# Mixture of experts on one core: the row gathers move from beside the first products to behind the output steps

## The chip, the cores and the metric

The kernel runs on one core of a Trainium2 chip. The metric is the device time of one execution in microseconds (us). Its engines are TensorE (PE in the profile; PEld are its weight loads), VectorE (DVE), ScalarE (ACT), GpSimd (POOL) and SyncE (SP). SP issues the plain DMAs, POOL the indirect ones, which gather or scatter rows by a list of indices.

## The reference, cut to what matters

Three layers follow each other: a linear attention, a dense two-layer network, and a mixture of 8 experts of which each of 2304 tokens takes two. The change lies in the last one.

```python
N, D, E, F = (2304, 512, 8, 1024)
noisy_logits = x @ w_gate + np.log1p(np.exp(x @ w_noise)) * noise
top2 = ...            # the two largest of the 8, and their softmax weights top2_w
out = np.zeros((N, D))
for e in range(E):
    for k in range(2):
        mask = top2[:, k] == e
        h = np.maximum(x[mask] @ w1[e], 0.0)
        out[mask] += top2_w[mask, k, None] * (h @ w2[e])
```

## The kernel before

The attention and the dense layer run first, in groups of 512 tokens. Their result, the token rows x, is written to a DRAM buffer `x2d`. While they run, the router of each group writes every token's number and weight into the list of its expert (36 small indirect DMAs, line 799, each followed by a memset named spacer). An expert's list has a capacity of CAP = 640 tokens, five blocks of 128.

The expert stage then works through the experts in order, lines 1095 to 1124. All products are float32 made of three float32r matmuls (`mm3`, lines 170 to 175): high x high, high x low, low x high. For expert e there are two phases.

- *First products* (`h2_step`, lines 888 to 904): for each of eight f, 128 hidden units by 640 tokens, as two parts of 384 and 256 columns with 12 matmuls each. They go to one of two PSUM buffers (`py`, tag Y). ACT writes the high part of the activated product to `hTh` (line 902), DVE the low part to `hTl` (line 903). PE's product f+2 needs the buffer of product f, so it waits for both.
- *Output steps* (`y2_step`, lines 908 to 927): for each block j of 128 tokens, 24 matmuls of 512 columns into one of two PSUM accumulators (`pa`, tag A). ACT scales them by the token's weight into a tile `y2s` (line 916), and POOL adds that tile to the output rows with an indirect DMA (line 917) and then writes the spacer (line 919).

Rows come in by `gather` (line 862). For experts 2 to 7 a block of 128 tokens takes four indirect DMAs on POOL (line 866), each of 128 rows of 512 bytes, into a tile of the pool `gp`, which has six buffers. `gtrans` (line 875) transposes a block on DVE and splits it into high and low (ACT line 885, DVE line 161). The transposition of expert e+1's block j stands ahead of expert e's output step j (line 1118), so the rows of expert e+1 are used in the output phase of expert e.

The program's order is written out by hand (`manual_schedule`), and each engine runs its own instructions in that order. At the top of expert e's turn stand the 20 gathers of expert e+1 (lines 1097 to 1099) and the loads of w1 for expert e+1 (SP, line 818); then the eight first products, with the split of w2 behind every second one; then the loads of w2 for expert e+1 (SP, line 822); then the five output steps. On POOL this gives, for each expert, 20 gathers in one run and then five pairs of scatter and spacer, each pair waiting for its output step. A scatter of expert e also waits for the adds of expert e-1 to land (lines 924 to 926).

Of the kernel before, what the change touches and what calls it, by code (L numbers as in the profile page):

```python
# [38 lines left out]
def attn_moe_moe2_kernel(  # L39
# [19 lines left out]
    E, _, F2 = w1.shape  # L59
# [10 lines left out]
    NB = CAP // P  # L70
# [80 lines left out]
    def GG(shape, dt, name):  # L151
        return gp.tile(shape, dt, tag="G", name=name)

    def TT(shape, dt, name):
        return tp.tile(shape, dt, tag="T", name=name)
# [14 lines left out]
    def mm3(out_ap, stat, mov, ssl, msl, start, stop):  # L170
        sh, sl = stat
        mh, ml = mov
        nc.tensor.matmul(out_ap, sh[ssl], mh[msl], start=start, stop=False)  # L173
        nc.tensor.matmul(out_ap, sh[ssl], ml[msl], start=False, stop=False)  # L174
        nc.tensor.matmul(out_ap, sl[ssl], mh[msl], start=False, stop=stop)  # L175
# [640 lines left out]
    def load_w1(e, i):  # L816
        raw1[e, i] = (HH if e == 0 else SS)([P, F2], F32, f"w1_{e}_{i}")
        nc.sync.dma_start(out=raw1[e, i], in_=quads(w1[e], i) if e >= NE else w1[e, i * P:(i + 1) * P, :])

    def load_w2(e, i):  # L820
        raw2[e, i] = SS([P, 2, DM], F32, f"w2_{e}_{i}")
        nc.sync.dma_start(out=raw2[e, i], in_=w2[e, 2 * i * P:2 * (i + 1) * P, :].rearrange("(a p) c -> p a c", p=P))

    def split_w1(e, i):
        s1[e, i] = split(W, raw1[e, i], [P, F2], f"s1_{e}_{i}")

    def split_w2(e, i):
        s2[e, i] = split(W, raw2[e, i], [P, 2, DM], f"s2_{e}_{i}", nc.gpsimd if e == 0 and i < 2 else None)
# [33 lines left out]
    def gather(e, j):  # L862
        if e >= NE:
            t = GG([P, NQ, P], F32, f"xg{e}_{j}")
            for g in range(NQ):
                nc.gpsimd.indirect_dma_start(out=t[:, g, :], out_offset=None, in_=x2d.rearrange("n (i c) -> (n i) c", c=P),  # L866
                                             in_offset=bass.IndirectOffsetOnAxis(ap=lq[:, e - NE, j, g:g + 1], axis=0))
        else:
            t = (HH if e == 0 and j < EB else GG)([P, DM], F32, f"xg{e}_{j}")
            rows = P + (groups[-1][0] if j < EB else NT)  # L870
            nc.gpsimd.indirect_dma_start(out=t, out_offset=None, in_=x2d[0:rows, :],
                                         in_offset=bass.IndirectOffsetOnAxis(ap=lst[:, e, j, 2:3], axis=0))
        xg[e, j] = t

    def gtrans(e, j):
        if j == 0:
            xgT[e] = (XX([P, NPR, CAP], F32R, f"xgh{e}"), XX([P, NPR, CAP], F32R, f"xgl{e}"))
        if e >= NE:
            t = quarters_transposed(xg[e, j], f"xgt{e}_{j}")
        else:  # L880
            t = MM([P, NPR, P], f"xgp{e}_{j}")
            for c in range(NPR):
                nc.tensor.transpose(t[:, c, :], xg[e, j][:, c * P:(c + 1) * P], ident)
        hi, lo = (u[:, :, j * P:(j + 1) * P] for u in xgT[e])
        nc.scalar.copy(hi, t)
        split_lo(lo, t, hi)

    def h2_step(e, f, parts=HALVES):
        if len(parts) == 2:
            ps = py.tile([P, 2, DM], F32, tag="Y", name=f"h2_{e}_{f}")  # L890
            banks = [ps[:, i, :] for i in range(2)]
        else:
            banks = [pa.tile([P, DM], F32, tag="A", name=f"h2_{e}_{f}_{parts[0][0]}")]
        for (a, n), bk in zip(parts, banks):
            for c in range(NPR):
                mm3(bk[:, :n], s1[e, c], xgT[e], (slice(None), slice(f * P, (f + 1) * P)),
                    (slice(None), c, slice(a, a + n)), c == 0, c == NPR - 1)
        if (e, f // 2) not in hT:
            hT[e, f // 2] = (HH([P, 2, CAP], F32R, f"hTh{e}_{f}"), HH([P, 2, CAP], F32R, f"hTl{e}_{f}"))
        for (a, n), bk in zip(parts, banks):  # L900
            hi, lo = (t[:, f % 2, a:a + n] for t in hT[e, f // 2])
            nc.scalar.activation(hi, bk[:, :n], AF.Relu)  # L902
            nc.vector.scalar_tensor_tensor(out=lo, in0=bk[:, :n], scalar=0.0, in1=hi.bitcast(F32),  # L903
                                           op0=ALU.max, op1=ALU.subtract)
# [3 lines left out]
    def y2_step(e, j, between={}):  # L908
        ps = pa.tile([P, DM], F32, tag="A", name=f"y2_{e}_{j}")
        for f in range(NF2):  # L910
            mm3(ps, tuple(t[:, f % 2] for t in hT[e, f // 2]), s2[e, f // 2], (slice(None), slice(j * P, (j + 1) * P)), (slice(None), f % 2),
                f == 0, f == NF2 - 1)
            if f in between:
                between[f]()
        t = TT([P, DM], F32, f"y2s{e}_{j}")
        nc.scalar.activation(t, ps, AF.Copy, scale=lst[:, e, j, 1:2].bitcast(F32))  # L916
        i = nc.gpsimd.indirect_dma_start(out=out, out_offset=bass.IndirectOffsetOnAxis(ap=lst[:, e, j, 0:1], axis=0),  # L917
                                         in_=t, in_offset=None, compute_op=ALU.add)
        nc.gpsimd.memset(spacer, 0)


        for o in adds.get(e, []):
            tc.declare_no_dep(i.ins, o.ins, reason="a token has one slot of an expert")
        for o in adds.get(e - 1, []):
            tc.add_manual_dep(i.ins, o.ins.name, mybir.DependencyInfo(mybir.DependencyClass.Sync, mybir.DependencyReason.DATA),
                              reason="adds to the same rows")
        adds.setdefault(e, []).append(i)


    with tc.manual_schedule():  # L930
# [164 lines left out]
        for e in range(E):  # L1095
            nx = e + 1 < E
            if nx and e:
                for j in range(NB):
                    gather(e + 1, j)
                for i in range(NPR):  # L1100
                    load_w1(e + 1, i)
            for f in range(NF2):
                h2_step(e, f, HALVES if e else PARTS[1:])
                if e and f % 2 == 0:
                    split_w2(e, f // 2)
                if e == 0 and f % 2:
                    gtrans(1, f // 2)
            if nx:
                for i in range(NF2 // 2):
                    load_w2(e + 1, i)  # L1110
            for j in range(NB):
                if e == 0 and j < EB - 1:
                    continue
                if nx:
                    if e:
                        if j < NPR:
                            split_w1(e + 1, j)
                        gtrans(e + 1, j)
                    elif j == EB - 1:
                        for i in range(NPR):  # L1120
                            split_w1(1, i)
                    else:
                        gtrans(1, j)
                y2_step(e, j)
    work.close()


# [69 lines left out]
```

## Time and profile before

| what | us |
|---|---|
| median of 3 runs | 1051.83 |
| lowest and highest of them | 1051.07, 1052.28 |
| the profiled execution's own time | 1058.36 |
| its span, first to last instruction | 1056.7 |
| mean granted TensorE clock in it | 0.952 of full speed |

| engine | busy us | share | instructions |
|---|---|---|---|
| PE | 968.6 | 92% | 4897 |
| DVE | 553.7 | 52% | 978 |
| ACT | 427.1 | 40% | 688 |
| POOL | 293.9 | 28% | 342 |

How to read it: a row of a timeline gives an instruction's start, its duration, the engine, the line of the kernel, the operation, what it writes and reads, and in square brackets the idle time of the engine ahead of it with what ended that idle time. "issue" there means that the profile shows nothing that the engine waited for, "remote" that an unknown one released it. The ends of matmuls are modelled. A row of the table of stretches gives, for each engine, its busy time in the stretch and the number of its instructions, then the granted clock (1.00 is 2.4 GHz), the busy share of the DMA engines and the GB/s that they moved.

### The profile page before, as it was taken

The page shows a single profiled execution, that of the slowest core. Times are in us where ns is not written, and L with a number is a line of the kernel's source. Part 1 is how long each engine was busy: PE and PEld are TensorE (multiplying, and loading weights), DVE is VectorE, ACT ScalarE, POOL GpSimd, SP SyncE. Part 2 cuts the span into 40 slices and gives each one's busy share as a digit, 9 for nine tenths or more (in the row PEclk, how much of TensorE's full clock was granted, in tenths as well). Part 3 has the DMA queues.
Part 4 walks back from the last instruction along what each step waited for, and adds up shares of the span by engine and source line. Part 5 has one row for each costly group of instructions (what it writes and reads, how often), then busy time and mean ns, then how long its engine had stood idle before and what let it go on. Part 6 is the DMA issues. An engine that isn't in the chain of part 4 may idle for free.

```text
span 1056.7 us, 12905 instructions
## 1 busy us (share of the span) xinstructions
PE 968.6 (92%) x4897; PEld 818.0 (77%) x4897; DVE 553.7 (52%) x978; ACT 427.1 (40%) x688; POOL 293.9 (28%) x342
## 2 busy tenths in 40 slices
PE   7989799999999999999999599697996997969994
PEld 7457578888888888898789499686886886868993
DVE  7899947964795567568434143242432523325320
ACT  3756544634463445467424132232331422314320
POOL 4002100150024003106342515427145162361111
PEclk8999899999999999999999799899898998989998
DMA  7688508600800120030652335244252442522203
GB/s 208 199 234 210 68 1 190 209 2 18 177 17 1 46 55 1 1 120 22 239 137 70 120 85 125 70 117 113 71 120 80 113 127 62 126 92 61 31 11 41
DMA packets 107282, 100.08 MB, mean 95 GB/s; under 512 B 58320, under 2 KB 82896, under 8 KB 107216
## 3 DMA queue, kind: packets, MB, share of 16 engines
q1 hardware_dynamic: 95664, 78.17, 26.2%
q0 software_dynamic: 11552, 21.04, 10.6%
q8 instruction: 40, 0.66, 0.3%
q14 instruction: 26, 0.21, 0.1%
HBM read 78.46 MB, written 20.72 MB: 94 GB/s over the span
## 4 chain that ended last, share of the span: by engine, by line
PE 74%; DVE 9%; issue 6%; another core or an unknown queue 5%; ACT 4%; DMA 1%; POOL 0%; DVEq 0%; POOLq 0%; SPq 0%; ACTq 0%
PE y L174 12%; PE y L173 12%; PE y L175 12%; PE h L175 11%; PE h L173 11%; PE h L174 10%; PE xp L495 2%; DVE stage L566 2%; ACT hTh L902 1%; PE kvp L381 1%; DVE hTl L903 1%; DVE stage L565 1%; PE qTp L482 1%; DVE hs L613 1%
## 5 line engine op out<-in xcount | busy, mean ns | idle before, releaser
L903 DVE SCALAR_TENSOR_TENSOR hTl<-h,hTh 128x384 fp32r<-128x384 f32 (+3 forms) x128 | 62.8, 491 | 233.7 <-ACT hTh L902 168.3
L902 ACT ACTIVATE hTh<-h 128x384 fp32r<-128x384 f32 (+3 forms) x128 | 56.0, 438 | 228.4 <-PE h L175 83.2
L917 POOL DMA_INDIRECT out_dram<-y2s,lst x40 | 63.3, 1581 | 282.9 <-ACT y2s L916 282.6
L866 POOL DMA_INDIRECT xg<-x2d,lq x120 | 118.9, 991 | 35.9 <-issue 33.1
L613 DVE SCALAR_TENSOR_TENSOR hs<-hs 128x512 f32<-128x512 f32 (+1 forms) x80 | 55.2, 690 | 54.5 <-ACT hs L612 52.7
L173 PE MATMUL h<-xgh,s_0h 128*128 128x384 f32 (+3 forms) x128 | 43.9, 343 | 43.1 <-DVE hTl L903 25.0
L438 POOL TENSOR_TENSOR q<-q,qm 128x1024 f32<-128x1024 f32 (+1 forms) x10 | 18.2, 1818 | 209.3 <-DVE qm L437 132.0
L612 ACT COPY hs<-h 128x512 f32<-128x512 f32 (+1 forms) x80 | 43.3, 541 | 76.7 <-PE h L175 73.1
L916 ACT ACTIVATE y2s<-y,lst 128x512 f32<-128x512 f32 x40 | 27.6, 689 | 91.3 <-PE y L175 76.4
L799 POOL DMA_INDIRECT lstd<-rrow,rsi x36 | 43.3, 1201 | 67.5 <-DVE rsi L796 61.6
L173 PEld LDWEIGHTS h<-xgh,s_0h 128*128 128x128 f32 x128 | 25.7, 201 | 46.9 <-DVE hTl L903 27.8
L624 ACT CAST g<-hs 128x512 fp32r<-128x512 f32 (+1 forms) x72 | 41.3, 573 | 37.8 <-DVE hs L613 37.7
L161 DVE TENSOR_TENSOR g<-hs,g 128x512 fp32r<-128x512 f32 (+1 forms) x72 | 44.9, 624 | 0.5 <-ACT g L624 0.5
L175 PE MATMUL h<-xgh,s_3l 128*128 128x384 f32 (+3 forms) x128 | 41.2, 322 | 2.9 <-issue 2.6
L175 PE MATMUL h<-xgh,s_0l 128*128 128x384 f32 (+3 forms) x128 | 41.9, 327 | 1.9 <-issue 1.9
L173 PE MATMUL h<-xgh,s_1h 128*128 128x384 f32 (+3 forms) x128 | 41.8, 327 | 1.7 <-issue 1.5
L174 PE MATMUL h<-xgl,s_0h 128*128 128x384 f32 (+3 forms) x128 | 42.1, 329 | 1.3 <-issue 1.3
L174 PE MATMUL h<-xgl,s_2h 128*128 128x384 f32 (+3 forms) x128 | 41.6, 325 | 1.1 <-issue 1.1
L173 PE MATMUL h<-xgh,s_2h 128*128 128x384 f32 (+3 forms) x128 | 41.4, 323 | 1.3 <-issue 1.3
L175 PE MATMUL h<-xgh,s_1l 128*128 128x384 f32 (+3 forms) x128 | 41.3, 323 | 1.3 <-issue 1.3
L174 PE MATMUL h<-xgl,s_1h 128*128 128x384 f32 (+3 forms) x128 | 41.5, 324 | 0.9 <-issue 0.8
L175 PE MATMUL h<-xgh,s_2l 128*128 128x384 f32 (+3 forms) x128 | 41.5, 324 | 0.6 <-issue 0.6
(341 smaller groups left out, 2914.4 us busy)
## 6 DMA issues: line engine op xcount, KB each, us to landing
w<-in_moe_w_dram SPq DMA_DIRECT2D x64, 512.0 KB
stage<-in_moe_w_in_dram SPq DMA_DIRECT2D x16, 512.0 KB
stage<-in_moe_w_out_dram SPq DMA_DIRECT2D x16, 512.0 KB
out_dram<-zero SPq DMA_DIRECT2D x1, 4864.0 KB
x2d<-x2s SPq DMA_DIRECT2D x9, 512.0 KB
k<-in_k_dram SPq DMA_DIRECT2D x12, 256.0 KB
v<-in_v_dram SPq DMA_DIRECT2D x12, 256.0 KB
x2q<-x2d SPq DMA_DIRECT2D x24, 128.0 KB
```

What stands on the lines that cost most here:

```text
L161: (eng or nc.vector).tensor_tensor(out=lo, in0=src, in1=hi.bitcast(F32), op=ALU.subtract)
L173: nc.tensor.matmul(out_ap, sh[ssl], mh[msl], start=start, stop=False)
L174: nc.tensor.matmul(out_ap, sh[ssl], ml[msl], start=False, stop=False)
L175: nc.tensor.matmul(out_ap, sl[ssl], mh[msl], start=False, stop=stop)
L612: nc.scalar.copy(hs, ps)
L613: nc.vector.scalar_tensor_tensor(out=hs, in0=hs, scalar=0.01, in1=hs, op0=ALU.mult, op1=ALU.max)
L624: nc.scalar.copy(parts[0], hs)
L799: i = nc.gpsimd.indirect_dma_start(out=lstd, out_offset=bass.IndirectOffsetOnAxis(ap=si[:, kk, r:r + 1], axis=0), in_=row[:, kk, r, :], in ...
L866: nc.gpsimd.indirect_dma_start(out=t[:, g, :], out_offset=None, in_=x2d.rearrange("n (i c) -> (n i) c", c=P), in_offset=bass.IndirectOffse ...
L902: nc.scalar.activation(hi, bk[:, :n], AF.Relu)
L903: nc.vector.scalar_tensor_tensor(out=lo, in0=bk[:, :n], scalar=0.0, in1=hi.bitcast(F32), op0=ALU.max, op1=ALU.subtract)
L917: i = nc.gpsimd.indirect_dma_start(out=out, out_offset=bass.IndirectOffsetOnAxis(ap=lst[:, e, j, 0:1], axis=0), in_=t, in_offset=None, com ...
```

## The change

The gathers of expert 2 stay where they were, at the top of expert 1's turn. Those of expert e+2, for e from 1 to 5, are issued in expert e's output phase instead of at the top of the turn of expert e+1: the four gathers of block j stand behind output step j of expert e, that is behind its scatter and spacer on POOL. Nothing else moves.

```diff
         for e in range(E):
             nx = e + 1 < E
             if nx and e:
-                for j in range(NB):
-                    gather(e + 1, j)
+                if e == 1:
+                    for j in range(NB):
+                        gather(2, j)
                 for i in range(NPR):
                     load_w1(e + 1, i)
             for f in range(NF2):
...
                     else:
                         gtrans(1, j)
                 y2_step(e, j)
+                if e and e + 2 < E:
+                    gather(e + 2, j)
     work.close()
```

## Rows read from the trace of the kernel before

**Rows 1.** The page: span, busy time by engine, and the evacuation of an output step.
```profile
span 1056.7 us, 12905 instructions
PE 968.6 (92%) x4897; PEld 818.0 (77%) x4897; DVE 553.7 (52%) x978; ACT 427.1 (40%) x688; POOL 293.9 (28%) x342
...
L916 ACT ACTIVATE y2s<-y,lst 128x512 f32<-128x512 f32 x40 | 27.6, 689 | 91.3 <-PE y L175 76.4
```

**Rows 2.** Table of stretches, each from one expert's first output scatter to the next's.
```profile
625.28:693.50 68.22, 59.01 (x314) 53.25 (x313) 24.15 (x34) 20.83 (x35) 28.54 (x30) 0.92 0.39 100
...
899.03:967.29 68.26, 58.91 (x314) 52.80 (x313) 24.14 (x34) 20.84 (x35) 28.41 (x30) 0.92 0.38 99
967.29:1022.65 55.36, 55.36 (x314) 50.66 (x313) 21.69 (x31) 19.11 (x32) 8.51 (x11) 1.00 0.18 25
sum 397.37, PE 351.73 PEld 317.07 DVE 142.41 ACT 123.40 POOL 150.72; mean PE 58.62 PEld 52.85 DVE 23.74 ACT 20.57 POOL 25.12
```

**Rows 3.** Timeline of ACT: three first products of expert 3, high part.
```profile
726.00 0.49 ACT L902 ACTIVATE hTh<-h 128x384 fp32r<-128x384 f32 x1 [3.22 <-PE h L175]
...
738.17 0.49 ACT L902 ACTIVATE hTh<-h 128x384 fp32r<-128x384 f32 x1 [9.73 <-issue]
...
746.03 0.49 ACT L902 ACTIVATE hTh<-h 128x384 fp32r<-128x384 f32 x1 [6.36 <-remote]
```

**Rows 4.** Timeline of PE: last matmuls of products four and five, first of six.
```profile
727.99 0.28 PE L175 MATMUL h<-xgh,s_3l 128*128 128x256 f32 x1
...
733.17 0.28 PE L175 MATMUL h<-xgh,s_3l 128*128 128x256 f32 x1
740.18 0.69 PE L173 MATMUL h<-xgh,s_0h 128*128 128x384 f32 x1 [6.73 <-DVE hTl L903]
```

**Rows 5.** Timeline of ACT: two first products of expert 7.
```profile
998.59 0.49 ACT L902 ACTIVATE hTh<-h 128x384 fp32r<-128x384 f32 x1 [2.01 <-PE h L175]
...
1002.10 0.49 ACT L902 ACTIVATE hTh<-h 128x384 fp32r<-128x384 f32 x1 [1.08 <-PE h L175]
```

**Rows 6.** Table of stretches: PE's pause in expert 3.
```profile
736.00:738.00 2.00, 0.00 (x0) 0.00 (x0) 0.00 (x0) 0.00 (x0) 1.70 (x2) 0.50 0.23 66
```

**Rows 7.** Timeline of POOL: scatters of expert 2, then the gathers for expert 4.
```profile
698.93 1.58 POOL L917 DMA_INDIRECT out_dram<-y2s,lst  x1 [3.69 <-ACT y2s L916]
...
704.37 1.56 POOL L917 DMA_INDIRECT out_dram<-y2s,lst  x1 [3.74 <-ACT y2s L916]
...
715.43 1.58 POOL L917 DMA_INDIRECT out_dram<-y2s,lst  x1 [3.94 <-ACT y2s L916]
...
722.59 0.95 POOL L866 DMA_INDIRECT xg<-x2d,lq  x1 [0.30 <-DVE hTl L903]
...
742.07 0.94 POOL L866 DMA_INDIRECT xg<-x2d,lq  x1 [0.30 <-issue]
```

**Rows 8.** Timelines of ACT and POOL: expert 1's late product; expert 6's last gather, late product.
```profile
604.60 0.49 ACT L902 ACTIVATE hTh<-h 128x384 fp32r<-128x384 f32 x1 [14.52 <-remote]
...
947.43 0.94 POOL L866 DMA_INDIRECT xg<-x2d,lq  x1 [0.30 <-issue]
...
951.44 0.49 ACT L902 ACTIVATE hTh<-h 128x384 fp32r<-128x384 f32 x1 [5.70 <-remote]
```

**Rows 9.** Timelines of SP and ACT: a load of w2 in expert 4, and a product.
```profile
818.75 0.37 SPq L822 DMA_DIRECT2D w<-in_moe_w_dram  x1
...
824.37 0.49 ACT L902 ACTIVATE hTh<-h 128x384 fp32r<-128x384 f32 x1 [1.08 <-PE h L175]
```

**Rows 10.** Timelines of POOL and ACT in the dense layer: eight list scatters, the products beside.
```profile
414.12 0.99 POOL L799 DMA_INDIRECT lstd<-rrow,rsi  x1 [4.02 <-DVE rsi L796]
...
423.77 0.96 POOL L799 DMA_INDIRECT lstd<-rrow,rsi  x1 [0.19 <-issue]
...
419.83 0.59 ACT L612 COPY hs<-h 128x512 f32<-128x512 f32 x1 [2.86 <-PE h L175]
...
425.27 0.59 ACT L612 COPY hs<-h 128x512 f32<-128x512 f32 x1 [3.39 <-issue]
```

## The prediction

> **What bounds the kernel now.** I read the page's busy shares first: TensorE (PE) is busy 92% of 1056.7 us, so either less PE work or fewer PE pauses can shorten the kernel [rows 1]. The change leaves the PE work alone, so the question is where PE pauses. The table of stretches answers it [rows 2]. I cut the expert stage at the first output scatter of each expert. Each of the six stretches then holds the same 314 matmuls: output steps 1 to 4 of one expert, the eight first products of the next, and its output step 0. The five that end with experts 2 to 6 take 397.37 - 55.36 = 342.01 us together (68.22 the first, 68.26 the fifth). The one that ends with expert 7 takes 55.36 us, with PE busy all through and the clock at 1.00 instead of 0.92. The five are longer by 342.01 - 5 x 55.36 = 65.2 us, 13.0 us for each expert. That is the stake.
>
> The timelines place the 13 us in the first products. In expert 3, PE ends the fourth product at 728.27 and the fifth at 733.45 (modelled ends), and then stands still for 6.73 us until 740.18 [rows 4], because both buffers of products are full. ACT, which empties them, starts on these two only at 738.17 and 746.03, after idle times of 9.73 and 6.36 us [rows 3]. By the program it needs only the finished product, and it starts 9.9 and 12.6 us after PE's end. In expert 7 ACT takes the products on the beat, 3.51 us apart [rows 5]. In PE's pause its clock falls to 1.2 GHz (0.50) [rows 6]; that loss is inside the 13 us.
>
> What stands beside the late products is POOL's run of 20 gathers. It begins behind the scatter of 715.43, does not pause, and ends at 743.01 (the fifth gather starts at 722.59, the twentieth at 742.07, 1.30 us apart in the mean) [rows 7]. ACT is released at 746.03, 3.02 us after the run's end. In expert 6 it is the same: the last gather ends at 948.37, ACT is released at 951.44, 3.07 us later [rows 8]. Expert 1, beside which expert 2's gathers run, shows it too: 14.52 us of ACT idle before 604.60 [rows 8]. Expert 7 has no gathers beside it and no pause. The weight loads are the other candidate. One is issued at 818.75, after the run of gathers beside expert 4, and ACT's product at 824.37 has 1.08 us of idle time ahead, as the one of 1002.10 in expert 7 has [rows 5, 9]; so a load alone does not do it.
>
> **The change part by part.** It adds and removes no instruction. Of 120 gathers, 100 (20 for each of experts 3 to 7) leave the place ahead of the first products of experts 2 to 6 and stand in groups of four behind the scatters of experts 1 to 5. The 20 for expert 2 stay beside expert 1, and so does that stall.
>
> *Removed.* If the run of gathers is what holds the products, the five stretches fall to the 55.36 us of the undisturbed one: -65.2 us [rows 2]. Nothing else is then late: that stretch holds the same evacuations, and PE is busy all through it. It lacks the weight loads; each load has an output phase or more until its use.
>
> *Added on POOL.* Scatter, spacer memset and four gathers took from 715.43 to the next start at 722.59, 7.16 us [rows 7]. The output steps come every 5.44 us (698.93 to 704.37) [rows 7]. POOL therefore falls behind by 1.72 us a step, and five groups end 35.8 us after the first scatter. For expert 2's steps, the first scatter is one step ahead of 698.93, at 693.5, and the end 729.3. Expert 3's first products began four products of 3.51 us ahead of 728.27, at 714.2. So 15.1 us of the stream still lie beside first products; today the run ends 28.8 us inside. What queues behind the gathers on POOL is only the next scatter. Who waits for that is ACT, which uses a scaled output tile again two steps later: scatter 2 is through POOL 16 us after scatter 0 began (2 x 7.16 + 1.6), and ACT wants its tile at 21, so 5 us are left for the landing. I take no cost; a longer landing would make ACT wait, and rival 1 has room for that. The scatters of the next expert, which wait for these to land, come 55 us later. The gathers' own consumer, DVE's transposition, gets them a whole expert earlier. The sixth buffer takes the first new gather, and each later one finds a buffer that DVE emptied one step before, so no wait is added.
>
> *The unknown: the same gathers beside output steps.* The trace shows no such stream. From below: eight indirect DMAs ran from 414.12 to 424.73, one every 1.38 us between starts, beside matmuls of the same 512 columns, and ACT took the product within and the one behind them at 419.83 and 425.27, 5.44 us apart [rows 10]. So a cost of 0 is possible at a density (8 in 10.6 us) a little above that of the new stream (5 in 7.16 us). From above: the 9.9 to 12.6 us of lateness in the first products [rows 3, 4]; rival 2 works that out. I take 0 for the output steps, as the row with the same matmul width and density is the nearer. For the tail beside the first products I take between 0 and the 1.2 us by which the third product of expert 3 was late, early in the run (PE's end 728.27 - 3.51 = 724.76, ACT at 726.00 [rows 3, 4]): 0.6 us an expert, 3 us in all.
>
> *Queues and weights.* SP's loads keep their places. The DMA engines are busy 0.38 to 0.39 of the long stretches [rows 2], and a move of 20 x 64 KB an expert within them does not bring them near 1.
>
> **Sum.** -65.2 + 3 = -62 us. The profiled execution took 1058.36 us (span 1056.7 and 1.7 around it), the median of the runs is 1051.83. I carry the difference over whole: 1051.83 - 62 = 990 us.
>
> **Rivals.**
> 1. *Half of it comes back.* The stream might hold PE's signals again once it has run for some gathers, and it reaches 15.1 us into the first products. At worst nothing is released there until 15.1 + 3.0 = 18.1 us; PE fills its two buffers in 7.0 us and stands for 11.1, so 11.1 of 13.0 us stay. At best 0. The middle, 5.5 us, leaves 7.5 x 5 = 37 us of gain: 1015 us. For it speaks that POOL really does not pause; against it that rows 10 show a stream of 10.6 us without harm.
> 2. *The stall comes along and grows: slower.* An output step has two accumulators. If each signal of PE is late by L, step j+2 starts L + 0.69 us after the end of step j instead of 5.44 us; 0.69 is the evacuation [rows 1]. With L = 12.6 us that is 7.9 us twice an expert, 15.7 us against the 13.0 saved: 2.7 x 5 = 14 us slower, 1065 us. It decides from L = 11.3 us on. If the tail kept its stall as well, the loss would be up to 79 us. For it speaks that 25 DMAs instead of 20 stand in one run; against it that a late signal delays the next scatter, which makes POOL pause and so ends the cause.
> 3. *The gathers are not the cause.* Then nothing changes: 1052 us. For it speaks that weight loads fall into the same stretches and that expert 7 has neither; against it that six experts with a run of gathers beside them have the pause, and that the release follows the last gather by 3.0 and 3.1 us in the two read [rows 3, 7, 8]. The Trainium skill's page "SBUF — State Buffer", section "Who interferes with whom", says that a DMA never contends with a compute engine and that PE waits on no one; by it this rival would be the rule, and the time 1052 us. The trace does not bear that out: PE's signals are late beside the long runs of gathers alone.
>
> **How the numbers follow.** Forecast 0.46 (984 to 1000 us), rival 1 0.30 (1000 to 1047), rival 2 0.15 (over 1054), rival 3 0.09. The range runs from 984 us (all of 65.2 and 3 us of spread) to 1052 us; it holds the forecast, rival 1 and a part of rival 3. A difference under 0.2%, some 2 us, is what a measurement here cannot tell from none: faster 0.77, same 0.08, slower 0.15.
>
> **What the changed kernel's profile would show.** Right: the five stretches near 55 to 57 us, PE busy all through with the clock at 1.00; ACT's starts in the first products 3.51 us apart; groups of scatter, memset and four gathers 7.16 us long, the last of them some 15 us into the next first products; expert 1's stall unchanged. Rival 1: ACT idle for PE in the third to fifth first product until 3 us behind the last gather. Rival 2: ACT's scaling of the outputs starts many us after PE's end, and PE pauses between output steps. Wrong altogether: no gathers beside the first products, and ACT still 10 us late.

## The result and the profile after

The changed kernel takes 999.39 us, the median of four runs (991.89 to 1009.41), against 1052.05 us before on the same chip. The ratio is 0.947, 95% interval 0.940 to 0.955; it leaves out the run of 1009.41 us, 1.8% above the fastest, as a slow one (the ratio of the two medians is 0.950). The forecast was 990 us, with a range of 984 to 1052. Its profiled execution took 995.28 us, 63.1 us less than the 1058.36 of before; the forecast was 62 us less. The runs now lie 17.5 us apart, before 4.1 us.

The page of the changed kernel, span and busy time by engine; it answers to [rows 1]:

```profile
span 993.6 us, 12904 instructions
PE 950.9 (96%) x4897; PEld 805.8 (81%) x4897; DVE 553.8 (56%) x978; ACT 427.3 (43%) x688; POOL 302.1 (30%) x342
```

The table of stretches, cut as in [rows 2], with expert 1's stretch, from expert 0's last scatter on, ahead of them and the five changed ones also as one (columns: window, its length, busy time and instructions of PE, PEld, DVE, ACT and POOL, TensorE's clock, DMA share, GB/s):

```profile
574.66:625.52 50.86, 40.00 (x215) 36.95 (x214) 15.28 (x23) 13.16 (x24) 20.74 (x23) 0.80 0.36 103
625.52:680.93 55.41, 55.41 (x314) 50.72 (x313) 24.23 (x34) 20.93 (x35) 30.36 (x31) 1.00 0.48 123
680.93:737.60 56.67, 55.89 (x314) 50.79 (x313) 24.29 (x34) 20.93 (x35) 29.58 (x30) 1.00 0.46 122
...
904.39:959.74 55.35, 55.35 (x314) 50.65 (x313) 21.70 (x31) 19.09 (x32) 8.51 (x11) 1.00 0.18 25
...
625.52:904.39 278.87, 278.06 (x1562) 253.67 (x1561) 121.27 (x170) 104.64 (x171) 150.93 (x150) 1.00 0.47 123
```

The five took 342.01 us and take 278.87: 63.1 us, the whole difference of the two profiles. Five undisturbed ones would take 5 x 55.35 = 276.8, so 2.1 us of stall are left, 1.3 of them in the stretch of expert 3. Expert 1 still has its stall: 50.86 us at a clock of 0.80. Its product waits as in [rows 8]:

```profile
604.88 0.49 ACT L902 ACTIVATE hTh<-h 128x384 fp32r<-128x384 f32 x1 [14.45 <-remote]
```

The timeline of ACT in expert 3, the last scaled output of expert 2 and three first products, the second to the fourth; it answers to [rows 3]:

```profile
705.04 0.69 ACT L916 ACTIVATE y2s<-y,lst 128x512 f32<-128x512 f32 x1 [6.88 <-issue]
...
710.89 0.49 ACT L902 ACTIVATE hTh<-h 128x384 fp32r<-128x384 f32 x1 [2.67 <-remote]
...
713.84 0.49 ACT L902 ACTIVATE hTh<-h 128x384 fp32r<-128x384 f32 x1 [1.45 <-remote]
...
718.23 0.49 ACT L902 ACTIVATE hTh<-h 128x384 fp32r<-128x384 f32 x1 [1.96 <-remote]
```

Idle times of 9.73 and 6.36 us have become 1.5 to 2.7. The products still come up to 2.2 us after PE's end (710.89), which PE's two buffers nearly cover: in the five stretches PE waits once, 0.7 us, for such a product, and never for an output step. New is the first line: ACT has nothing to scale into. ACT's waits, summed over experts 1 to 6 (us in total, times, longest), say what it lacks, a scatter's landing:

```profile
ACT y2s L916 <- DMA out_dram<-y2s,lst: 30.4, 6, 7.1
```

The timeline of POOL beside these output steps, scatters and the last gather; it answers to [rows 7]:

```profile
680.93 1.62 POOL L917 DMA_INDIRECT out_dram<-y2s,lst  x1 [18.30 <-ACT y2s L916]
...
687.89 1.88 POOL L917 DMA_INDIRECT out_dram<-y2s,lst  x1 [0.30 <-issue]
...
710.60 1.63 POOL L917 DMA_INDIRECT out_dram<-y2s,lst  x1 [0.30 <-issue]
...
716.31 0.94 POOL L866 DMA_INDIRECT xg<-x2d,lq  x1 [0.30 <-issue]
```

Four groups take 710.60 - 680.93 = 29.67 us, 7.42 each, and the stream ends 36.3 us after its start. POOL never waits in it. From the first scatter's start to the last gather's there are 24 steps in 35.38 us, 1.47 us a DMA in the mean; in [rows 7] it is 1.33 us, 20 steps from the scatter at 715.43 to 742.07. A stream of 36 us without a pause does little harm, then, where one of 26 us stalled PE. Why, the experiments had to say.

### The profile page after: what moved, and what is told of

Read it like the earlier page. It is cut to its first block, busy times and chain, and to the rows that moved or that the text cites. A ratio compares the mean times of both kernels' runs of the same rounds, so it can differ in the third digit from the quotient of the medians.

```text
span 993.6 us, 12904 instructions
## 1 busy us (share of the span) xinstructions
PE 950.9 (96%) x4897; PEld 805.8 (81%) x4897; DVE 553.8 (56%) x978; ACT 427.3 (43%) x688; POOL 302.1 (30%) x342
## 3 DMA queue, kind: packets, MB, share of 16 engines
q0 software_dynamic: 11552, 21.04, 11.3%
## 4 chain that ended last, share of the span: by engine, by line
PE 82%; DVE 6%; ACT 3%; DMA 2%; another core or an unknown queue 2%; issue 2%; SPq 0%; POOL 0%; POOLq 0%; DVEq 0%; ACTq 0%
PE h L173 13%; PE h L175 13%; PE y L173 13%; PE y L174 13%; PE h L174 13%; PE y L175 13%; PE xp L495 2%; PE kvp L381 1%; DVE stage L566 1%; PE qTp L482 1%; DVE stage L565 1%; DMA q<-in_q_dram 1%; DVE hs L613 1%; DMA stage<-in_moe_w_in_dram 1%
## 5 line engine op out<-in xcount | busy, mean ns | idle before, releaser
L866 POOL DMA_INDIRECT xg<-x2d,lq x120 | 125.1, 1043 | 33.6 <-issue 32.0
L917 POOL DMA_INDIRECT out_dram<-y2s,lst x40 | 65.7, 1642 | 213.5 <-ACT y2s L916 207.1
L173 PE MATMUL h<-xgh,s_0h 128*128 128x384 f32 (+3 forms) x128 | 41.5, 324 | 5.1 <-issue 3.4
L173 PE MATMUL h<-xgh,s_3h 128*128 128x384 f32 (+3 forms) x128 | 40.2, 314 | 0.0
L174 PE MATMUL h<-xgl,s_3h 128*128 128x384 f32 (+3 forms) x128 | 40.2, 314 | 0.0
```

## The experiments

Twelve kernels ran, in four groups, each group on one chip beside the kernel before, which took 1054.02 us beside e1 to e4, 1066.81 beside e5 to e8, 975.88 beside e9 to e11 and 1053.12 beside e12. The third of these numbers is itself a result. All fences of this section are tables of stretches with the columns above, first expert 1's, then the five as one, unless the text says otherwise.

**e1: two gathers behind each first product, with a wait.** From the kernel before:

```diff
-                for j in range(NB):
-                    gather(e + 1, j)
+                if e == 1:
+                    for j in range(NB):
+                        gather(2, j)
...
                 h2_step(e, f, HALVES if e else PARTS[1:])
+                if nx and e > 1:
+                    pace(e, f)      # POOL copies one column of hTh
+                    gather_part(e + 1, 2 * f)
+                    gather_part(e + 1, 2 * f + 1)
...
                 y2_step(e, j)
+                if nx and e > 1 and j == 0:
+                    for n in range(2 * NF2, NB * NQ):
+                        gather_part(e + 1, n)
```

> The kernel before, with the gathers for experts 3 to 7 still beside the first products of the expert in front, but no longer in one run: two behind each first product, after a one-column copy on POOL that waits for ACT's evacuation of that product, and the last four behind output step 0. Theory (a long run of POOL's gathers without a pause holds back PE's signals; a run with pauses does not): the stall goes although the gathers stay beside the first products; the five stretches that took 342.0 us before and 278.9 us in the changed kernel take 277 to 292 us. Rival A (the phase matters: the short matmuls of the first products don't stand gathers beside them): each expert keeps at least half of its 13 us, 310 us or more.

Measured 990.2 us, ratio 0.938 (0.932 to 0.944).

```profile
575.29:622.15 46.86, 36.29 (x215) 33.92 (x214) 15.21 (x23) 13.30 (x24) 21.72 (x23) 0.89 0.41 113
622.15:898.97 276.82, 276.82 (x1562) 253.31 (x1561) 121.28 (x170) 104.77 (x171) 166.83 (x186) 1.00 0.48 123
```

The gathers are back beside the first products, PE is busy all through at full clock, and the five stretches are at the undisturbed 276.8. Place alone is not the cause. Rival A falls.

**e2: five gathers of whole rows. e3: plain transfers from SP. e4: a quarter of the bytes.** Each replaces the gathers of line 866 in the kernel before:

```diff
-                nc.gpsimd.indirect_dma_start(out=t[:, g, :], out_offset=None, in_=x2d.rearrange("n (i c) -> (n i) c", c=P),
-                                             in_offset=bass.IndirectOffsetOnAxis(ap=lq[:, e - NE, j, g:g + 1], axis=0))
# e2, once for a block instead of four times
+            nc.gpsimd.indirect_dma_start(out=t.rearrange("p g c -> p (g c)"), out_offset=None, in_=x2d[0:P + NT, :],
+                                         in_offset=bass.IndirectOffsetOnAxis(ap=lst[:, e, j, 2:3], axis=0))
# e3
+                nc.sync.dma_start(out=t[:, g, :], in_=x2d[(j + 1) * P:(j + 2) * P, g * P:(g + 1) * P])
# e4 (the transposition then reads the 32 columns four times; its line is left out here)
+                nc.gpsimd.indirect_dma_start(out=t[:, g, 0:32], out_offset=None, in_=x2d.rearrange("n (i c) -> (n i) c", c=32),
+                                             in_offset=bass.IndirectOffsetOnAxis(ap=lq[:, e - NE, j, g:g + 1], axis=0))
```

> The kernel before, with five gathers of whole rows of 2 KB for each of experts 2 to 7 in place of twenty gathers of quarter rows of 512 B, at the same place and with the same bytes (the rows then stand in another order in the tile, so those experts compute on other columns). Theory (length of POOL's run): the run falls from 26 us to some 7 us, the five stretches take 277 to 285 us, and expert 1's stretch falls from 51.0 to some 38 us. Rival B (the bytes or the transfers themselves beside the first products): no change, some 342 us.

> The kernel before, with the twenty gathers for each of experts 2 to 7 replaced at the same place by twenty plain transfers of 128 pieces of 512 B from SP's queue (fixed rows, so those experts compute on other tokens). Theory (POOL's own run is what holds the signals): no stall, the five stretches take 277 to 290 us. Rival B (DMA traffic of 512 B pieces beside the first products, whoever issues it): 330 us or more.

> The kernel before, with each of the twenty gathers cut from 512 B to 128 B a row at the same place (the transposition reads the 32 columns four times, so experts 2 to 7 compute on other columns). A quarter of the bytes, the same number of gathers and of row pieces. Theory (number of gathers in the run, not bytes): the stall stays, the five stretches take 330 to 342 us. Rival B (bytes): a quarter of the stall or less, under 300 us.

Measured 971.47 us (0.919), 972.76 us (0.921) and 1057.67 us (1.002, 0.999 to 1.006). e2:

```profile
573.50:606.77 33.27, 33.27 (x215) 32.12 (x214) 15.30 (x23) 13.29 (x24) 6.59 (x7) 1.00 0.55 159
606.77:883.59 276.82, 276.82 (x1562) 253.34 (x1561) 121.17 (x170) 104.62 (x171) 68.34 (x75) 1.00 0.47 124
```

e3:

```profile
606.06:882.89 276.83, 276.83 (x1562) 253.33 (x1561) 121.17 (x170) 104.63 (x171) 41.79 (x51) 1.00 0.52 123
```

e4:

```profile
619.18:962.63 343.45, 295.86 (x1562) 268.54 (x1561) 120.73 (x170) 104.29 (x171) 142.74 (x151) 0.92 0.35 86
```

The matmuls and the work of DVE and ACT are the same, as the counts show, but on other columns or rows, so none of the three is a kernel to use. With the same bytes in few gathers, or in plain transfers, there is no stall, and expert 1's goes too (33.27 us in e2). With a quarter of the bytes in as many gathers the stall is whole (1.5 us over the range expected). It is POOL's many gathers, not the traffic; whether their number, the age of the run or its rate counts was still open.

**e5: a short instruction between the gathers.** Behind each gather of the kernel before:

```diff
+                nc.gpsimd.memset(spacer, 0)
```

> The kernel before with one instruction more behind each of the twenty gathers of experts 2 to 7: the one-column memset that stands behind each output scatter and each list scatter already. The gathers stay in one run at the same place, and POOL still doesn't wait. Theory (any stream of POOL's DMAs that dense, beside first products, holds the signals): the stall stays, the five stretches take 325 to 360 us. Rival C (it is gathers issued back to back, with no other POOL instruction between them, that do it; this would explain why the eight list scatters and the new stream of scatter, memset, four gathers do no harm): 277 to 295 us.

Measured 1076.44 us, ratio 1.013 (1.005 to 1.022). The table, and the timeline of POOL in expert 2's run:

```profile
623.26:984.56 361.30, 299.06 (x1562) 268.71 (x1561) 120.95 (x170) 104.22 (x171) 153.48 (x251) 0.89 0.37 95
...
654.91 0.95 POOL L866 DMA_INDIRECT xg<-x2d,lq  x1 [0.19 <-issue]
655.86 0.11 POOL L868 MEMSET spacer<- 128x1 int32 x1
656.16 0.95 POOL L866 DMA_INDIRECT xg<-x2d,lq  x1 [0.19 <-issue]
```

The memset took 0.11 us of the 0.30 us that stood idle behind each gather anyway: the gathers still started 1.25 us apart, and the stall stayed, 1.3 us over the range expected. Another instruction between them does nothing by itself; rival C falls.

**e6: 12 of the 20 gathers stay.** From the changed kernel:

```diff
+                for j in range(2, NB if e > 1 else 0):
+                    gather(e + 1, j)
...
-                if e and e + 2 < E:
+                if e and e + 2 < E and j < 2:
                     gather(e + 2, j)
```

> The changed kernel with only two of five blocks (8 gathers) of experts 4 to 7 moved behind output steps; the other 12 stay in a run beside the first products, as before. Theory (signals are held until 3 us behind the last gather of the run, and PE's two product buffers and its work in hand cover the first part): 8 gathers fewer at 1.30 us end the hold 10.4 us sooner, which leaves 13.0 - 10.4 = 2.6 us for each of these four experts; each of the four stretches that had 68 us takes 56 to 60 us. Rival D (every gather costs PE the same): 12/20 of 13.0 = 7.8 us stay, 63 us each.

Measured 1007.38 us.

```profile
625.31:914.72 289.41, 281.32 (x1562) 256.41 (x1561) 120.99 (x170) 104.50 (x171) 149.36 (x151) 0.99 0.48 118
```

The five stretches (five, not four: the expectation miscounted) are 289.41 - 276.8 = 12.6 us too long, 2.5 each; expected were 2.6, by rival D 7.8. One of them alone has 7.3, the others 0.8 to 2.0, so the mean fits better than the single ones. The one with 7.3 has the densest run, 1.33 us a DMA in the mean from the scatter ahead of it to its last gather; the others have 1.40 to 1.45. That the first gathers of a run are free fits this, but the run of 12 does not show it by itself.

**e7: the whole run behind output step 1.** From the changed kernel:

```diff
-                        gtrans(e + 1, j)
+                        for n in ((0, 1, 2), (3, 4))[j] if j < 2 else ():
+                            gtrans(e + 1, n)
...
-                if e and e + 2 < E:
-                    gather(e + 2, j)
+                if e and e + 2 < E and j == 1:
+                    for n in range(NB):
+                        gather(e + 2, n)
```

> The changed kernel with all twenty gathers of experts 3 to 7 in one run behind output step 1 of the expert two in front (the transpositions of the next expert's five blocks are taken forward to output steps 0 and 1 to free the buffers), so that some 16 us of the 26 us run stand beside the output steps 2 to 4 and 10 us beside first products; the scatters of steps 2 to 4 queue behind the run. Theory (beside the 512-column matmuls of output steps the run does no harm): ACT takes the products of steps 2 to 4 on the beat, 5.4 us apart, and at most 3 us are lost beside the first products: stretches of 55.4 to 59 us. Rival C or D (the run itself does it, wherever it stands): ACT's scalings in steps 3 and 4 or the first products come 5 to 12 us late, and the stretches take 63 us or more.

Measured 1091.31 us, ratio 1.025 (1.017 to 1.033). Timeline of POOL in expert 2: the scatter of output step 1, the first and the last gather, the last scatter behind them:

```profile
712.26 1.57 POOL L917 DMA_INDIRECT out_dram<-y2s,lst  x1 [4.38 <-ACT y2s L916]
...
714.13 1.01 POOL L866 DMA_INDIRECT xg<-x2d,lq  x1 [0.19 <-issue]
...
738.12 0.94 POOL L866 DMA_INDIRECT xg<-x2d,lq  x1 [0.30 <-issue]
...
743.20 1.57 POOL L917 DMA_INDIRECT out_dram<-y2s,lst  x1 [0.19 <-issue]
```

Timeline of ACT in the same time, the fifth output step and the first product behind it:

```profile
723.60 0.69 ACT L916 ACTIVATE y2s<-y,lst 128x512 f32<-128x512 f32 x1 [4.69 <-DMA xg<-x2d,lq]
743.96 0.49 ACT L902 ACTIVATE hTh<-h 128x384 fp32r<-128x384 f32 x1 [19.68 <-remote]
```

This kernel is the slowest of all. The output steps beside the run are on the beat (712.82, 718.22, 723.60), but the last of them comes only 11.3 us after the scatter that heads the run; the next product, the first of expert 3, is taken after 19.7 us of idle time. In the kernel before, too, products were taken within 1.2 us until 726.00, 10.6 us after the scatter at 715.43 [rows 3, 7]. In both the lateness sets in some 11 us into the run, whether its first gathers stand beside output steps or first products. My theory that output steps protect the gathers, which gave at most 59 us a stretch, falls: they took 371.99 / 5 = 74.4. What an output step that came later in so dense a run would suffer, e7 does not show.

**e8: one more scaled-output tile.** From the changed kernel:

```diff
-    gp = work.enter_context(tc.tile_pool(name="gp", bufs=6))
-    tp = work.enter_context(tc.tile_pool(name="tp", bufs=4))
+    gp = work.enter_context(tc.tile_pool(name="gp", bufs=5))
+    tp = work.enter_context(tc.tile_pool(name="tp", bufs=5))
...
```

> The changed kernel with five scaled-output tiles instead of four (and five gather buffers instead of six, expert 1's fifth block gathered later, to make room). It tells what the new wait costs, ACT's scaling waiting up to 6.9 us for a scatter to land. If that wait costs the 0.1 to 1.3 us by which each of the five stretches is over 55.35 us: they fall from 278.9 to 277 to 277.5 us, and the spread of the runs (991.9 to 1009.4 us) shrinks. If the wait is covered and the spread comes from elsewhere: 278 to 280 us and the same spread.

Measured 997.42 us (994.98 to 1006.13), ratio 0.936 (0.929 to 0.942).

```profile
623.65:915.05 291.40, 282.64 (x1562) 258.15 (x1561) 121.62 (x170) 104.96 (x171) 149.42 (x151) 0.98 0.46 118
```

Neither expectation: the scalings are on the beat in this profile, 5.44 us apart, so the wait is gone but for one of 1.3 us, yet the stretches are 12.5 us longer than in the changed kernel's profile, in three of the five experts (6.4, 4.2 and 4.1 us), where PE's signals for first products are late again. So the lateness comes without the wait. The two times come from two chips and say nothing of the wait's cost; that PE never waited for an output step in the changed kernel's profile does.

**e9 and e10: spacing without waits. e11: the paced form everywhere.** e9 and e10 put one or two memsets of 256 columns behind each gather of the kernel before; e11 is e1 without the exception for expert 2:

```diff
+                nc.gpsimd.memset(kvs[0][:, 0:2, :], 0.0)      # e9; e10 twice
...
-                if nx and e > 1:
+                if nx and e:                                   # e11
...
```

> The kernel before with a memset of 256 columns behind each of the twenty gathers of experts 2 to 7 (no wait; it only takes time). The gathers then start some 1.46 us apart instead of 1.25 to 1.30, about as dense as the new stream of the changed kernel (five DMAs in 7.16 us, 1.43 us each); the run lasts 29 us, all beside first products. Theory E (rate: POOL must not start DMAs closer than some 1.4 us for longer than 9 to 10 us): little or no stall, the five stretches take 277 to 300 us. Rival F (age of the run: PE's signals are held from 9 to 10 us after POOL's first gather until 3 to 5 us behind the last, as long as POOL never waits): the run is longer, so the stall too, 342 us or more. Rival G (output steps are what protects the stream of the changed kernel): 342 us.

> The same with two such memsets: gathers some 1.78 us apart, as dense as the paced form (two in 3.5 us, 1.75 us each), but POOL never waits; the run lasts 36 us and reaches beyond the first products. Theory E (rate): no stall, 276.8 to 280 us for the five stretches (up to 8 us more for the scatters that queue behind the run, if ACT should wait for them). Rival F (age): 360 us or more. If this one is free and the 1.46 us form is not, the bound lies between 1.46 and 1.78 us, and the changed kernel's stream owes its freedom to more than its rate.

> The paced form (two gathers behind each first product, after a copy that waits for ACT's evacuation) for expert 2's gathers too, which beside expert 1 were one run in all kernels but e2 and e3. Expert 1's stretch falls from 46.9 us to the 33.3 us that it has without a run, which is 13.6 us: 990.2 - 13.6 = 976.6 us, and no stall is left that belongs to the gathers. If the spread of the runs comes from those stalls, the runs lie within 5 us of each other.

Measured 976.27 us, 986.8 us and 976.23 us; ratios 1.001 (0.999 to 1.003), 1.011 (1.008 to 1.014) and 1.000 (0.998 to 1.001). On this chip the kernel before takes 975.88 us, so these three can't tell the theories apart: there is hardly a stall to remove. e10 shows what a run that is too long costs by itself:

```profile
607.28:894.89 287.61, 279.68 (x1562) 253.99 (x1561) 121.11 (x170) 104.71 (x171) 211.77 (x348) 0.99 0.48 119
```

That is 2.2 us an expert (287.61 - 276.8 = 10.8 for five), since the scatters queue behind the gathers and ACT waits for them.

**e12: the forms side by side, in one kernel.** Expert 1 as in e11, 2 as before, 3 as in e9, 4 as in e10, 5 with two runs of 10, and expert 7's gathers as in the changed kernel:

```diff
-                for j in range(NB):
-                    gather(e + 1, j)
+                for n in range({2: 20, 3: 20, 4: 20, 5: 10}.get(e, 0)):
+                    gather_part(e + 1, n)
+                    for _ in range({3: 1, 4: 2}.get(e, 0)):
+                        nc.gpsimd.memset(kvs[0][:, 0:2, :], 0.0)
...
+                if e == 5 and f == 3:
+                    pace(e, f)
+                    for n in range(10, NB * NQ):
+                        gather_part(e + 1, n)
...
+                if e == 5:
+                    gather(e + 2, j)
```

> One kernel with another form beside each expert, so that one trace compares them on one chip: beside expert 1's first products the paced form, beside expert 2's the one run of 20 as before (the control), beside 3's the run with one memset of 256 columns behind each gather (1.46 us apart), beside 4's with two (1.78 us apart), beside 5's two runs of 10, the second of which waits for ACT's fourth product; expert 7's gathers in the changed kernel's form, behind expert 5's output steps. If the control shows no stall (55.4 us), as the kernel before on the chip of e9 to e11, nothing is told apart but the changed form's own cost. If it stalls (67 to 75 us): expert 1's stretch is 33.3 us. Theory E (rate: DMAs started closer than some 1.4 us for longer than 9 to 10 us): the third stretch 55.4 to 58 us, the fourth 57 us (ACT waits for late scatters, as in e10), the fifth 55.4 to 59 us, the one with expert 7's stream 55.4 to 56.7 us. Rival F (age of the run while POOL never waits): third and fourth 68 us or more, fifth 55.4 to 60 us. Rival H (the number of gathers beside the products, however spread): third and fifth 66 us or more.

Measured 1003.43 us beside 1053.12, ratio 0.952 (0.949 to 0.955): a chip with the stall. The table of stretches, each from ACT's scaling of a first output (the first window: of expert 0's last) to that of the next expert:

```profile
576.27:609.54 33.27, 33.27 (x215) 32.30 (x215) 15.07 (x23) 13.03 (x23) 23.31 (x26) 1.00 0.55 150
609.54:679.65 70.11, 59.21 (x314) 53.69 (x313) 24.20 (x35) 20.86 (x34) 32.88 (x34) 0.90 0.40 102
679.65:735.02 55.37, 55.37 (x314) 50.67 (x313) 24.25 (x35) 20.95 (x34) 35.95 (x49) 1.00 0.48 123
735.02:790.37 55.35, 55.35 (x314) 50.65 (x313) 24.27 (x35) 20.95 (x34) 36.07 (x60) 1.00 0.47 120
790.37:850.95 60.58, 57.65 (x321) 52.10 (x320) 23.68 (x34) 20.75 (x35) 36.27 (x44) 1.00 0.48 119
850.95:913.68 62.73, 57.05 (x306) 51.85 (x306) 24.74 (x35) 20.72 (x35) 28.23 (x30) 0.95 0.42 109
913.68:969.02 55.34, 55.34 (x314) 50.64 (x313) 21.87 (x32) 19.39 (x32) 8.50 (x10) 1.00 0.19 25
```

Timelines of POOL: the scatter ahead of the control's run and its last gather; in expert 3 the same, with two gathers of its run between:

```profile
632.32 1.56 POOL L928 DMA_INDIRECT out_dram<-y2s,lst  x1 [3.76 <-ACT y2s L927]
...
659.25 0.95 POOL L880 DMA_INDIRECT xg<-x2d,lq  x1 [0.30 <-issue]
...
702.57 1.58 POOL L928 DMA_INDIRECT out_dram<-y2s,lst  x1 [3.93 <-ACT y2s L927]
...
728.30 0.95 POOL L880 DMA_INDIRECT xg<-x2d,lq  x1 [0.16 <-issue]
...
729.75 0.96 POOL L880 DMA_INDIRECT xg<-x2d,lq  x1 [0.17 <-issue]
...
734.51 0.95 POOL L880 DMA_INDIRECT xg<-x2d,lq  x1 [0.16 <-issue]
```

The control stalls (70.11). With a memset behind each gather, in a run of over 30 us that never waits, nothing is lost (55.37; 55.35 with the two memsets of e10's form). That is two experts of one profile, beside their control. Rivals F (age) and H (number) fall; the rate decides, in runs as long as these. The usual step from gather to gather is 1.45 us there and 1.25 in the control. Some gathers take up to 2 us, however, so in the mean a DMA starts every (734.51 - 702.57) / 20 = 1.60 us there and every (659.25 - 632.32) / 20 = 1.35 us in the control; the bound lies between.

Two runs of 10 cost up to 5.2 us (60.58; late scatters of the run of e10's form ahead are in it) instead of 14.8, where theory E had a stretch of 59 us at most. They hardly were two: the eleventh gather started 2.8 us after the tenth, and the mean over both is 1.44 us. The changed kernel's own stream lost 62.73 - 55.35 = 7.4 us here, where theory E allowed 1.3: that part missed. It began 7.7 us behind the second run of 10, so it was not quite by itself.

The mean step, from the first scatter's start to the last gather's, puts all streams of the changed kernel's form in order, over three profiles: at 1.51 us they lost 0.0 to 0.2 us (three streams of the changed kernel's profile, two of e8's), at 1.47 to 1.48 us 0.3 to 4.2 us (two and two), at 1.46 us 6.4 us (e8), at 1.42 us 7.4 us (here). So the bound is near 1.5 us, and the changed kernel stands at it, not clear of it. Within a group its gathers are 1.25 us apart; whether the mean counts or the longer step at each scatter, no run tells.

## Why the prediction was right, step by step

*The stake*, 65.2 us for five stretches over 55.36, was right: e1, e2 and e3 reach 276.8 us, the undisturbed level, and 65.2 above it is what the kernel before had.

*Removed*, -65.2 us, with nothing else late behind it: right. e2, e3 and e4 show the cause as the prediction had it, POOL's run of gathers. Rival 3, that the gathers are not the cause, falls, and so does rival 2, since no output step kept PE waiting. The Trainium skill's page "SBUF — State Buffer" says under "Who interferes with whom" that a DMA never contends with a compute engine. As a rule for the time it fails here: the run of [rows 7] and e4's (343.45 us) held back PE's signals, while e3's transfers from SP (276.83 us) agree with it. The section is about SBUF's ports, and whether a port has any part in this no run shows.

*Added on POOL*, a lag of 1.72 us a step and an end after 35.8 us: measured 7.42 - 5.44 = 1.98 us and 36.3 us (up to 37.2 in the other experts). Right in the main; the 0.26 us by which a group took longer turned out to matter, as said below.

*"5 us are left for the landing. I take no cost"*: the slack was too thin. In expert 2 the scatter of output step 2 was through POOL at 697.72, and ACT wrote its tile again, for step 4, at 705.04, 7.3 us later; over all it waited for landings up to 7.1 us. The cost of none was right all the same: PE never waited for an output step in the five stretches.

*The unknown*, no cost beside output steps: the number held in the profile, the reason did not, and that was in part luck. I chose the value by matmul width and density together. e7 shows that gathers beside output steps count like the others, e12 that the density does it. The eight DMAs of [rows 10], 1.38 us apart, are denser than the stream that lost 7.4 us in e12; but their run ended after 10.6 us, about where lateness sets in elsewhere, so they were no neighbour for a stream of 36 us. Had the groups taken the 7.16 us reckoned, 1.43 us a DMA, the order of the streams in e12 would put the loss at some 5 to 7 us an expert, an estimate from 1.42 us (7.4 us lost), 1.44 us (5.2 at most) and 1.46 us (6.4 lost), which is rival 1's size.

*The tail*, 3 us: 2.1 us in the profile. In other executions it is more. The median gain is 52.7 us where the profiles have 63.1: the profiled execution of the kernel before lies 6.3 us above its median, that of the changed kernel 4.1 us below its own, so the close match of 63.1 to 62 is in part luck. The four runs spread over 17.5 us; e8 and e12 show the same stream losing 0 to 7.4 us an expert. That would make the 9.4 us by which the median lies above the forecast; the runs have no profiles of their own, so this is argued, not shown. For it speaks that e1, which has nothing left to lose in the five, gained 63.8 us in the medians (1054.02 to 990.2). Rival 1 had the mechanism (the stream does not pause and reaches the first products), with 37 us of gain; the truth lies between it and the forecast, nearer to the forecast.

*Expert 1 unchanged*: right, 14.45 us of idle time after 14.52. e11's form takes that stall away as well (33.27 us in e12).

What the prediction could not see is that all of this hangs on the chip. On that of e9 to e11 the kernel before has nothing to lose; the changed kernel was not run there.

*Better than both.* e1, 276.82 us for the five stretches, is at the floor, and its four runs vary less (989.24 to 994.84 us). It ran on another chip than the changed kernel, and the intervals of the two ratios, 0.938 and 0.947, overlap. With expert 2's gathers paced too (e11) it should take 990.2 - (46.86 - 33.27) = 976.6 us on a chip with the stall; it was only run on the one without, where it equals the kernel before.

## What to carry to other kernels

A stall beside a burst need not be cured by moving the burst: look at its rate first, since 0.25 us more between the DMAs in the mean, where they stood, left less of the stall (0.0 us an expert in e12) than moving them did (0.4 us an expert in its profile, 7.4 in e12). Count the rate over the whole run, since the usual step alone (1.25 or 1.45 us) hides the longer ones. An explanation by place ("beside output steps") and one by rate fit the same trace; a run of the full burst in the other place tells them apart. Compare only beside a control on the same chip, best inside the same kernel.

## What was not expected of the hardware

- On the chips of three groups POOL's gathers 1.25 us apart stall PE from some 11 us into their run on; on that of e9 to e11 the same kernel takes 975.88 us instead of 1053 to 1067. It is PE's signal that is late: for the product that ACT takes at 746.03 [rows 3], which PE ended at 733.45 by the model, the packed trace has the update of PE's semaphore at 746.01.
- The list of DMA issues (out and in, engine, count, us from issue to landing) gives the gathers a landing time on that chip only, here e11:

```profile
xg<-x2d,lq POOLq DMA_INDIRECT x120, 3.7
```

  In the changed kernel, on a chip with the stall, the line has none:

```profile
xg<-x2d,lq POOLq DMA_INDIRECT x120
```

  A part of the updates by which these DMAs tell of their landing is missing there. Counted in the packed traces, 1889 of the 3296 updates of POOL's 206 indirect DMAs (16 each) are missing before, 1529 in the changed kernel and 1166 in e1, but 8, 44 and 3 in e9, e10 and e11. That would fit updates, or the records of them, that pile up where PE's signals pass too. Missing updates alone make no stall: e2 lacks 480 of 1856 and has none. What the two share was not found; whether the recording of an execution has a part in the stall was not tested, and why one chip is spared stays open.
